# Four tokens per partition, input gate on GpSimd, scan input in fp32 PSUM: a gated linear recurrence on one core

## The chip, the cores and the metric

The kernel runs on one core of a Trainium2 chip. The metric is the device time of one execution in microseconds (us), the median of repeated runs. A profiled execution gives the views quoted here. Its span is some 2 us shorter than the time of the same run. The engines are PE (matmul), DVE (VectorE), ACT (ScalarE), POOL (GpSimd) and the 16 DMA engines; PEld is PE's weight load.

## The reference, cut to what matters

There are 4 sequences of 6336 tokens with 256 channels, in fp32.

```python
sig_r, sig_i = sigmoid(r_gate), sigmoid(i_gate)
a_t  = exp(8 * sig_r * log(a_base))                # decay per token and channel
xg   = sqrt(max(1 - a_t**2, 1e-6)) * sig_i * x
h    = a_t[:, t] * h + xg[:, t];  y[:, t] = h      # for every t
gate = sigmoid(causal_conv5(y))                    # 5 taps per channel
out  = (gate * (y @ w_val)) @ w_out
```

## The kernel before

The 25344 tokens are cut into 49 windows of 512 and one of 256. A window is loaded with tokens on partitions. PE transposes it so that channels lie on partitions and tokens along the row, and DVE then scans along the row. A static plan, made from a table of estimated durations (`COST`), fixes each engine's order. Rings of 11 windows lie between the front (load, tanh, exp, square) and the back (scan, convolution, output). The parts that matter here are:

```python
# load: token j*128 + p of the window goes to partition p: pieces of 1 KB
nc.sync.dma_start(dst, src[t0:t0 + nj * P, :].rearrange("(j p) d -> p j d", p=P))
...
# input gate, DVE: (tanh(i/2) + 1) * x, both operands in SBUF
nc.vector.scalar_tensor_tensor(out=uring[...], in0=tri[:, 1, ...], scalar=1.0, in1=xt[...], op0=ALU.add, op1=ALU.mult)
# square of the decay, GpSimd
nc.gpsimd.tensor_tensor(out=ering[...], in0=a, in1=a, op=ALU.mult)
# gating, DVE: transposed input (PSUM, bf16) times norm (SBUF, bf16) -> SBUF, bf16
nc.vector.tensor_tensor(out=xg[...], in0=uT[...], in1=nh[...], op=ALU.mult)
# scan, DVE, per half of the channels: decay (SBUF) and gated input (SBUF)
nc.vector.tensor_tensor_scan(out=yb[:, h, ...], data0=aring[...], data1=xg[:, h, c0:c1], initial=..., op0=ALU.mult, op1=ALU.add)
...
# final gate, DVE: (tanh + 1) * value, contiguous
nc.vector.scalar_tensor_tensor(out=gv[...], in0=tg[...], scalar=1.0, in1=val[...], op0=ALU.add, op1=ALU.mult)
# output product, PE: 128 tokens of gv are the weights
nc.tensor.matmul(out=ops[:, e, :], lhsT=gv[:, hk, p0:p0 + P], rhs=wo2[:, hk, :], ...)
```

## Time and profile before

| | before |
|---|---|
| time, median of the first 3 runs | 375.75 us (374.08 to 376.87) |
| span of the profiled run | 372.5 us |
| DVE, ACT, PE, POOL busy | 334.6, 312.4, 272.4, 138.3 us |
| DMA packets, share of 16 engines' span | 105160; main queue 85.7% |

The lines are shown in the prediction. In a group line the columns are the source line, engine, operation, output and input names with their shapes, and the count. After the first bar come the busy sum in us and the mean ns of one. After the second bar comes the engine's idle time just before these instructions, with what ended most of it. In the slice view each digit is the busy share of one fortieth of the span, in tenths.

### The profile page before, as it was taken

Reading aid. Unit: us, or ns where it says so; the run is one execution under the profiler, and the core shown is the slowest. Engines: PE = TensorE matmul, PEld = TensorE weight load, DVE = VectorE, ACT = ScalarE, POOL = GpSimd, SP = SyncE. Lnnn points to the kernel's source line nnn. Section 1 sums busy time; section 2 is a strip of 40 time slices with the busy share of each in tenths; the row PEclk is TensorE's granted clock in tenths of the full one; section 3 lists DMA queues with packets and bytes.
Section 4 is the critical chain, followed back from the end, with each engine's and each line's share of the span. In section 5 each row is a group of like instructions: output and inputs, shape, how many; then the busy total and the mean of one; then the engine's idle time right before and its main releaser. Section 6 shows DMA issues by size and latency. Waiting matters only on the chain.

```text
span 372.5 us, 5299 instructions
## 1 busy us (share of the span) xinstructions
PE 272.4 (73%) x1933; PEld 159.9 (43%) x1933; DVE 334.6 (90%) x326; ACT 312.4 (84%) x298; POOL 138.3 (37%) x111
## 2 busy tenths in 40 slices
PE   0362779877686969877677887696976696869994
PEld 0232445444445535434344454363543363435543
DVE  3363999999999979999999999999999999999982
ACT  4898899999998799998967989789997997873342
POOL 2234435634362726434425324451655056300000
PEclk9995699999899899999889989789999899999998
DMA  8999996999999989996889979979999895313333
GB/s 210 355 348 353 356 350 201 298 353 339 345 361 324 330 268 361 352 364 202 280 264 339 351 226 295 356 255 344 301 323 336 278 340 187 127 56 114 113 114 141
DMA packets 105160, 104.42 MB, mean 280 GB/s; under 512 B 3240, under 2 KB 105135, under 8 KB 105135
## 3 DMA queue, kind: packets, MB, share of 16 engines
q1 hardware_dynamic: 104590, 103.83, 85.7%
q0 software_dynamic: 544, 0.26, 0.5%
q8 instruction: 15, 0.25, 0.3%
q14 instruction: 11, 0.08, 0.1%
HBM read 78.39 MB, written 25.95 MB: 280 GB/s over the span
## 4 chain that ended last, share of the span: by engine, by line
DVE 34%; ACT 23%; issue 19%; PE 14%; DMA 5%; POOL 2%; DVEq 0%; ACTq 0%
DVE yring L306 13%; DVE uring L246 8%; DVE gv L344 7%; ACT tri L240 6%; ACT ering L277 5%; PE gp L321 5%; PE ops L356 4%; ACT aring L257 4%; DMA xt<-in_x_dram 3%; DVE xg L290 3%; PE val L338 3%; ACT tg L327 3%; DVE osb L367 2%; ACT L327 2%; ACT L277 2%
## 5 line engine op out<-in xcount | busy, mean ns | idle before, releaser
L262 POOL TENSOR_TENSOR ering<-aring 128x1024 f32<-128x1024 f32 (+1 forms) x50 | 105.7, 2121 | 140.9 <-ACT aring L257 121.8
L321 PE MATMUL gp<-yring,diag 128*128 128x512 bf16 (+4 forms) x530 | 124.5, 384 | 24.7 <-DVE yring L306 14.2
L306 DVE TENSOR_TENSOR_SCAN yring<-aring,yring,xg 128x512 bf16<-128x512 f32 (+4 forms) x98 | 139.5, 1464 | 0.7
L240 ACT ACTIVATE tri<-ri 128x2048 bf16<-128x2048 f32 (+1 forms) x50 | 94.4, 1907 | 0.0
L321 PEld LDWEIGHTS <-diag 128*128 128x128 bf16 x530 | 50.8, 102 | 83.5 <-issue 16.3
L356 PE MATMUL ops<-wo,gv 128*128 128x256 bf16 x396 | 61.8, 280 | 26.2 <-DVE gv L344 12.4
L257 ACT ACTIVATE aring<-srT,khf 128x512 f32<-128x512 bf16 (+1 forms) x100 | 71.8, 791 | 3.4 <-PE srT L228 2.2
L246 DVE SCALAR_TENSOR_TENSOR uring<-tri,xt 128x1024 bf16<-128x1024 bf16 (+1 forms) x50 | 67.4, 1356 | 7.0 <-ACT tri L240 6.9
L327 ACT ACTIVATE tg<-gp 128x1024 bf16<-128x1024 f32 (+1 forms) x50 | 51.1, 1023 | 25.7 <-PE gp L321 21.2
L344 DVE SCALAR_TENSOR_TENSOR gv<-tg,val 128x1024 bf16<-128x1024 bf16 (+1 forms) x50 | 59.7, 1194 | 2.5 <-PE val L338 1.7
L304 POOL COPY yring<-yring 128x8 bf16<-128x8 bf16 x49 | 31.6, 644 | 77.4 <-DVE yring L306 77.4
L356 PEld LDWEIGHTS <-gv 128*128 128x128 bf16 x396 | 36.7, 99 | 50.0 <-DVE gv L344 20.2
L338 PE MATMUL val<-yring,wv 128*128 128x512 bf16 (+4 forms) x212 | 52.1, 371 | 5.3 <-DVE gv L344 5.3
L228 PE MATMUL srT<-ident_b,tri 128*128 128x128 bf16 x396 | 33.4, 232 | 22.2 <-ACT tri L240 22.2
L277 ACT ACTIVATE ering<-ering,b 128x3072 bf16<-128x3072 f32 (+2 forms) x21 | 47.0, 2280 | 0.1
L369 ACT COPY osb<-ops 128x512 f32<-128x512 f32 x46 | 27.2, 592 | 22.2 <-PE ops L356 19.1
L367 DVE COPY osb<-ops 128x512 f32<-128x512 f32 x53 | 36.1, 682 | 9.2 <-PE ops L356 8.0
L228 PE MATMUL uT<-ident_b,uring 128*128 128x128 bf16 x396 | 33.3, 232 | 15.0 <-DVE xg L290 14.7
L228 PEld LDWEIGHTS <-tri 128*128 128x128 bf16 x396 | 27.0, 104 | 33.2 <-ACT tri L240 27.1
L290 DVE TENSOR_TENSOR xg<-uT,ering 128x1024 bf16<-128x1024 bf16 (+1 forms) x50 | 33.7, 675 | 6.2 <-ACT ering L277 6.2
L228 PEld LDWEIGHTS <-uring 128*128 128x128 bf16 x396 | 28.3, 104 | 20.0 <-issue 14.3
L338 PEld LDWEIGHTS <-wv 128*128 128x128 bf16 x212 | 19.9, 99 | 18.9 <-issue 6.6
(31 smaller groups left out, 53.3 us busy)
## 6 DMA issues: line engine op xcount, KB each, us to landing
ri<-in_r_gate_dram SPq DMA_DIRECT2D x49, 512.0 KB, 6.1
ri<-in_i_gate_dram SPq DMA_DIRECT2D x49, 512.0 KB, 7.4
xt<-in_x_dram SPq DMA_DIRECT2D x49, 512.0 KB, 7.3
out_dram<-osb SPq DMA_DIRECT2D x49, 512.0 KB, 4.6
ri<-in_r_gate_dram SPq DMA_DIRECT2D x1, 256.0 KB, 7.0
ri<-in_i_gate_dram SPq DMA_DIRECT2D x1, 256.0 KB, 7.2
xt<-in_x_dram SPq DMA_DIRECT2D x1, 256.0 KB, 6.6
out_dram<-osb SPq DMA_DIRECT2D x1, 256.0 KB
```

Of the source, the lines that this page charges most:

```text
L228: nc.tensor.transpose(out=dst[:, h, j * P:(j + 1) * P], in_=src[:, j, h * P:(h + 1) * P], identity=ident_b[:])
L240: nc.scalar.activation(out=tri[:, :, 0:nj, :], in_=ri[:, :, 0:nj, :], func=ACT.Tanh, scale=0.5)
L246: nc.vector.scalar_tensor_tensor(out=uring[:, g % NS, 0:nj, :], in0=tri[:, 1, 0:nj, :], scalar=1.0, in1=xt[:, 0:nj, :], op0=ALU.add, op1=A ...
L257: nc.scalar.activation(out=aring[:, g % NS, h, 0:ntok[g]], in_=srT[:, h, 0:ntok[g]], func=ACT.Exp, scale=khf[:, h:h + 1], bias=khf[:, h:h ...
L262: nc.gpsimd.tensor_tensor(out=ering[:, g % NS, :, 0:ntok[g]], in0=a, in1=a, op=ALU.mult)
L277: nc.scalar.activation(out=nring[:, sl:sl + k, 0:H * WIN], in_=ering[:, sl:sl + k].rearrange("p s h t -> p s (h t)"), func=ACT.Sqrt, scale ...
L306: nc.vector.tensor_tensor_scan(out=yb[:, h, o:o + c1 - c0], data0=aring[:, g % NS, h, c0:c1], data1=xg[:, h, c0:c1], initial=0.0 if fresh ...
L321: nc.tensor.matmul(out=gp[:, h, c0:c1], lhsT=diag[:, h, kk, :], rhs=yb[:, h, o:o + c1 - c0], start=(kk == 0), stop=(kk == CONV_K - 1))
L327: nc.scalar.activation(out=tg[:, :, 0:ntok[g]], in_=live.pop(("gp", g))[:, :, 0:ntok[g]], func=ACT.Tanh, scale=0.5)
L338: nc.tensor.matmul(out=val[:, m, c0:c1], lhsT=wv[:, hk, m * P:(m + 1) * P], rhs=yb[:, hk, o:o + c1 - c0], start=(hk == 0), stop=(hk == H - 1))
L344: nc.vector.scalar_tensor_tensor(out=gv[:, :, 0:ntok[g]], in0=live.pop(("tg", g))[:, :, 0:ntok[g]], scalar=1.0, in1=live.pop(("val", g))[: ...
L356: nc.tensor.matmul(out=ops[:, e, :], lhsT=gv[:, hk, p0:p0 + P], rhs=wo2[:, hk, :], start=(hk == 0), stop=(hk == H - 1))
```

## The change

The intent was to take the input gate off the fullest engine, to free the scan from its delays beside GpSimd (in the kernel before a pair of scans takes 4.04 us beside a square and 2.45 us with GpSimd idle), to load and store pieces of 4 KB, and to drop small copies at the ring's seams.

- Partition p now holds four successive tokens, so pieces are 4 KB. PE's transposes then deliver tokens permuted, and three later operations read or write with a step to put them in order and back.
- The input gate becomes two GpSimd instructions.
- The gating is split in halves and writes fp32 to PSUM, where the scan reads it.
- The y ring is contiguous, so the convolution reads over the seam and the four-column copies go.

```diff
-            nc.sync.dma_start(dst, src[...].rearrange("(j p) d -> p j d", p=P))
+            nc.sync.dma_start(dst, src[...].rearrange("(p j) d -> p j d", j=nj))
...
-            nc.vector.scalar_tensor_tensor(out=uring[...], in0=tri[:, 1, 0:nj, :], scalar=1.0,
-                                           in1=xt[:, 0:nj, :], op0=ALU.add, op1=ALU.mult)
+            t1 = work.tile([P, SUB, D], FP32, name="t1", tag="t1", bufs=1)
+            nc.gpsimd.tensor_scalar(out=t1[...], in0=tri[:, 1, 0:nj, :], scalar1=1.0, scalar2=None, op0=ALU.add)
+            nc.gpsimd.tensor_tensor(out=uring[...], in0=t1[...], in1=xt[...], op=ALU.mult)
...
-            srT = psum.tile([P, H, WIN], BF16, name="srT", tag="srT", bufs=2)
+            srT = psum.tile([P, H, WIN], BF16, name="srT", tag="srT", bufs=1)
...
+            for h in range(H):
+                xg = psum.tile([P, WIN], FP32, name="xg", tag="xg", bufs=1)
+                nc.vector.tensor_tensor(out=xg[...], in0=by_token(uT, h, g), in1=nring[...], op=ALU.mult)
...
-            gv = work.tile([P, H, WIN], BF16, name="gv", tag="gv", bufs=2)
-            nc.vector.scalar_tensor_tensor(out=gv[...], in0=tg[...], scalar=1.0, in1=val[...], ...)
+            gv = work.tile([P, SUB, H, P], BF16, name="gv", tag="gv", bufs=2)
+                nc.vector.scalar_tensor_tensor(
+                    out=gv[:, 0:nj, hs, :].rearrange("c j h p -> c (h p) j"),
+                    in0=tg[:, hs, ...].rearrange("c h (p j) -> c (h p) j", j=nj), scalar=1.0,
+                    in1=val[:, hs, ...].rearrange("c h (p j) -> c (h p) j", j=nj), op0=ALU.add, op1=ALU.mult)
```

Cut: the ring's index arithmetic, the split convolution at the seam, the load, store and exp patterns, and the new `COST` values.

More of the change, by code (lines that the diff above doesn't have):

```diff
@@ L19 @@
 MIN_UNIT = [1, 2, 3, 4]
-COST = dict(load=4.5, tanh=1.9, u2=1.3, srT=0.5, uT=0.5, exp=1.45, e=2.15, xg=0.66, scan=2.7, conv=2.4, tg=0.97,
-            val=0.95, gv=1.16, out=0.47, osbD=0.64, osbA=0.62, sq=0.88, sq0=0.2, table=1.3, store=1.5,
+COST = dict(load=3.9, tanh=1.9, u2=3.3, srT=0.5, uT=0.5, exp=1.45, e=2.15, scan=3.75, conv=2.45, tg=1.0,
+            val=0.95, gv=1.2, out=0.5, osbD=0.68, osbA=0.6, sq=0.88, sq0=0.2, table=1.3, store=1.3,
             sem=0.15, dma=2.2)
@@ L67, in make_plan @@
         per_window("tanh", "ACT", 3, [("load", 0), ("srT", -NTRI), ("u2", -NTRI)])
-        per_window("u2", "DVE", 0, [("tanh", 0), ("uT", -NS)])
-        per_window("srT", "PE", 0, [("tanh", 0), ("exp", -2)])
+        per_window("u2", "POOL", 1, [("tanh", 0), ("uT", -NS)])
+        per_window("srT", "PE", 0, [("tanh", 0), ("exp", -1)])
         per_window("exp", "ACT", 1, [("srT", 0), ("scan", -NS), ("e", -NS)])
-        per_window("e", "POOL", 0, [("exp", 0), ("xg", -NS)])
-        per_window("uT", "PE", 1, [("u2", 0), ("xg", -1)], nsq)
-        per_window("xg", "DVE", 3, [("uT", 0), ("sq", 0), ("scan", -1)], nsq)
-        per_window("scan", "DVE", 2, [("xg", 0), ("val", -NY)], nsq)
+        per_window("e", "POOL", 0, [("exp", 0), ("scan", -NS)])
+        per_window("uT", "PE", 1, [("u2", 0), ("scan", -1)], nsq)
+        per_window("scan", "DVE", 2, [("uT", 0), ("sq", 0), ("val", -NY), ("conv", 1 - NY)], nsq)
         per_window("conv", "PE", 3, [("scan", 0), ("tg", -1)])
@@ L97, in make_plan @@
                                               and at("exp") >= NS)
-            low = (nsq - at("scan")) * (COST["xg"] + COST["scan"]) <= 2 * COST["table"] + COST["sq"] * n
+            low = (nsq - at("scan")) * (COST["scan"]) <= 2 * COST["table"] + COST["sq"] * n
             enough = n >= min(MIN_UNIT[min(len(units), len(MIN_UNIT) - 1)], nw - nsq)
@@ L151 @@
         segs.append([(c0 - t0, c1 - t0, c0 % S == 0) for c0, c1 in zip(cuts[:-1], cuts[1:])])
-    YW = WIN + 4 * max(len(s) for s in segs)
     plan, qwin = make_plan([n / WIN for n in ntok])
@@ L165, in load @@
         for dst, src in ((ri[:, 0, 0:nj, :], rf), (ri[:, 1, 0:nj, :], if_), (xt[:, 0:nj, :], xf)):
-            nc.sync.dma_start(dst, src[t0:t0 + nj * P, :].rearrange("(j p) d -> p j d", p=P))
+            nc.sync.dma_start(dst, src[t0:t0 + nj * P, :].rearrange("(p j) d -> p j d", j=nj))
         live["ri", g], live["xt", g] = ri, xt
@@ L222 @@
         uring = rings.tile([P, NS, SUB, D], BF16, name="uring")
-        yring = rings.tile([P, NY, H, YW], BF16, name="yring")
+        yring = rings.tile([P, H, NY * WIN], BF16, name="yring")
         def transposes(dst, src, g):
@@ L245, in op_u2, with by_token @@
             xt, tri = live.pop(("xt", g)), live["tri", g]
-            nc.vector.scalar_tensor_tensor(out=uring[:, g % NS, 0:nj, :], in0=tri[:, 1, 0:nj, :], scalar=1.0,
-                                           in1=xt[:, 0:nj, :], op0=ALU.add, op1=ALU.mult)
+            t1 = work.tile([P, SUB, D], FP32, name="t1", tag="t1", bufs=1)
+            nc.gpsimd.tensor_scalar(out=t1[:, 0:nj, :], in0=tri[:, 1, 0:nj, :], scalar1=1.0, scalar2=None, op0=ALU.add)
+            nc.gpsimd.tensor_tensor(out=uring[:, g % NS, 0:nj, :], in0=t1[:, 0:nj, :], in1=xt[:, 0:nj, :],
+                                    op=ALU.mult)
         def op_srT(g, eng, n):
-            srT = psum.tile([P, H, WIN], BF16, name="srT", tag="srT", bufs=2)
+            srT = psum.tile([P, H, WIN], BF16, name="srT", tag="srT", bufs=1)
             transposes(srT, live["tri", g][:, 0], g)
             live["srT", g] = srT
+        def by_token(t, h, g):
+            return t[:, h, 0:ntok[g]].rearrange("c (j p) -> c p j", p=P)
         def op_exp(g, eng, n):
             srT = live.pop(("srT", g))
+            nj = ntok[g] // P
             for h in range(H):
-                nc.scalar.activation(out=aring[:, g % NS, h, 0:ntok[g]], in_=srT[:, h, 0:ntok[g]], func=ACT.Exp,
+                nc.scalar.activation(out=aring[:, g % NS, h, 0:ntok[g]].rearrange("c (p j) -> c p j", j=nj),
+                                     in_=by_token(srT, h, g), func=ACT.Exp,
                                      scale=khf[:, h:h + 1], bias=khf[:, h:h + 1])
@@ L285, in op_uT @@
             live["uT", g] = uT
-        def op_xg(g, eng, n):
-            xg = work.tile([P, H, WIN], BF16, name="xg", tag="xg", bufs=2)
-            nh = nring[:, g % NS, 0:H * WIN].rearrange("p (h t) -> p h t", h=H)
-            nc.vector.tensor_tensor(out=xg[:, :, 0:ntok[g]], in0=live.pop(("uT", g))[:, :, 0:ntok[g]],
-                                    in1=nh[:, :, 0:ntok[g]], op=ALU.mult)
-            live["xg", g] = xg
-        def op_scan(g, eng, n):
-            xg = live.pop(("xg", g))
-            yb = yring[:, g % NY]
-            py = yring[:, (g - 1) % NY]
-            pend = ntok[g - 1] + 4 * len(segs[g - 1]) if g else 0
-            for s, (c0, c1, fresh) in enumerate(segs[g]):
-                o = c0 + 4 + 4 * s
-                if fresh:
-                    nc.gpsimd.memset(yb[:, :, o - 4:o], 0.0)
-                else:
-                    nc.gpsimd.tensor_copy(out=yb[:, :, o - 4:o], in_=py[:, :, pend - 4:pend])
-                for h in range(H):
+        def op_scan(g, eng, n):
+            uT = live.pop(("uT", g))
+            nj = ntok[g] // P
+            y0 = g % NY * WIN
+            yp = (g - 1) % NY * WIN + (ntok[g - 1] if g else 0) - 1
+            for h in range(H):
+                xg = psum.tile([P, WIN], FP32, name="xg", tag="xg", bufs=1)
+                nc.vector.tensor_tensor(
+                    out=xg[:, 0:ntok[g]].rearrange("c (p j) -> c p j", j=nj), in0=by_token(uT, h, g),
+                    in1=nring[:, g % NS, h * WIN:h * WIN + ntok[g]].rearrange("c (p j) -> c p j", j=nj),
+                    op=ALU.mult)
+                for (c0, c1, fresh) in segs[g]:
                     nc.vector.tensor_tensor_scan(
-                        out=yb[:, h, o:o + c1 - c0],
+                        out=yring[:, h, y0 + c0:y0 + c1],
                         data0=aring[:, g % NS, h, c0:c1],
-                        data1=xg[:, h, c0:c1],
-                        initial=0.0 if fresh else py[:, h, pend - 1:pend],
+                        data1=xg[:, c0:c1],
+                        initial=0.0 if fresh else yring[:, h, yp:yp + 1],
                         op0=ALU.mult, op1=ALU.add,
@@ L314, in op_conv @@
         def op_conv(g, eng, n):
-            yb = yring[:, g % NY]
             gp = psum.tile([P, H, WIN], FP32, name="gp", tag="gp", bufs=1)
+            y0 = g % NY * WIN
+            yend = NY * WIN
             for h in range(H):
-                for s, (c0, c1, fresh) in enumerate(segs[g]):
-                    for kk in range(CONV_K):
-                        o = c0 + 4 * s + kk
-                        nc.tensor.matmul(out=gp[:, h, c0:c1], lhsT=diag[:, h, kk, :], rhs=yb[:, h, o:o + c1 - c0],
-                                         start=(kk == 0), stop=(kk == CONV_K - 1))
+                for kk in range(CONV_K - 1, -1, -1):
+                    sh = CONV_K - 1 - kk
+                    parts = []
+                    for (c0, c1, fresh) in segs[g]:
+                        if fresh:
+                            parts.append((c0 + sh, c1, y0 + c0))
+                        elif y0 + c0 >= sh:
+                            parts.append((c0, c1, y0 + c0 - sh))
+                        else:
+                            parts.append((0, sh, yend - sh))
+                            parts.append((sh, c1, y0))
+                    if sh == 0:
+                        parts = [(0, ntok[g], y0)]
+                    for k, (c0, c1, src) in enumerate(parts):
+                        nc.tensor.matmul(out=gp[:, h, c0:c1], lhsT=diag[:, h, kk, :],
+                                         rhs=yring[:, h, src:src + c1 - c0],
+                                         start=(sh == 0), stop=(kk == 0 and k == len(parts) - 1))
             live["gp", g] = gp
@@ L331, in op_val @@
         def op_val(g, eng, n):
-            yb = yring[:, g % NY]
+            y0 = g % NY * WIN
             val = psum.tile([P, H, WIN], FP32, name="val", tag="val", bufs=1)
             for m in range(H):
-                for s, (c0, c1, fresh) in enumerate(segs[g]):
-                    for hk in range(H):
-                        o = c0 + 4 * s + 4
-                        nc.tensor.matmul(out=val[:, m, c0:c1], lhsT=wv[:, hk, m * P:(m + 1) * P],
-                                         rhs=yb[:, hk, o:o + c1 - c0], start=(hk == 0), stop=(hk == H - 1))
+                for hk in range(H):
+                    nc.tensor.matmul(out=val[:, m, 0:ntok[g]], lhsT=wv[:, hk, m * P:(m + 1) * P],
+                                     rhs=yring[:, hk, y0:y0 + ntok[g]], start=(hk == 0), stop=(hk == H - 1))
             live["val", g] = val
         def op_gv(g, eng, n):
-            gv = work.tile([P, H, WIN], BF16, name="gv", tag="gv", bufs=2)
-            nc.vector.scalar_tensor_tensor(out=gv[:, :, 0:ntok[g]], in0=live.pop(("tg", g))[:, :, 0:ntok[g]],
-                                           scalar=1.0, in1=live.pop(("val", g))[:, :, 0:ntok[g]],
-                                           op0=ALU.add, op1=ALU.mult)
+            gv = work.tile([P, SUB, H, P], BF16, name="gv", tag="gv", bufs=2)
+            tg, val = live.pop(("tg", g)), live.pop(("val", g))
+            nj = ntok[g] // P
+            for hs in ([slice(0, H)] if nj == SUB else [slice(h, h + 1) for h in range(H)]):
+                nc.vector.scalar_tensor_tensor(
+                    out=gv[:, 0:nj, hs, :].rearrange("c j h p -> c (h p) j"),
+                    in0=tg[:, hs, 0:ntok[g]].rearrange("c h (p j) -> c (h p) j", j=nj), scalar=1.0,
+                    in1=val[:, hs, 0:ntok[g]].rearrange("c h (p j) -> c (h p) j", j=nj), op0=ALU.add, op1=ALU.mult)
             live["gv", g] = gv
@@ L353, in op_out @@
             for e in range(2):
-                p0 = (2 * i + e) * P
                 for hk in range(H):
-                    nc.tensor.matmul(out=ops[:, e, :], lhsT=gv[:, hk, p0:p0 + P], rhs=wo2[:, hk, :],
+                    nc.tensor.matmul(out=ops[:, e, :], lhsT=gv[:, 2 * i + e, hk, :], rhs=wo2[:, hk, :],
                                      start=(hk == 0), stop=(hk == H - 1))
@@ L372, in op_store @@
             nj = ntok[g] // P
-            nc.sync.dma_start(of[g * WIN:g * WIN + nj * P, :].rearrange("(j p) d -> p j d", p=P),
+            nc.sync.dma_start(of[g * WIN:g * WIN + nj * P, :].rearrange("(p j) d -> p j d", j=nj),
                               live.pop(("osb", g))[:, 0:nj, :])
         ops_by_name = dict(load=op_load, tanh=op_tanh, u2=op_u2, srT=op_srT, exp=op_exp, e=op_e, sq=op_sq,
-                           uT=op_uT, xg=op_xg, scan=op_scan, conv=op_conv, tg=op_tg, val=op_val, gv=op_gv,
+                           uT=op_uT, scan=op_scan, conv=op_conv, tg=op_tg, val=op_val, gv=op_gv,
                            out=op_out, osb=op_osb, store=op_store)
```

## The prediction

> **What bounds the kernel now.** I read the page's busy shares first, then the slices over time, then the groups by line, then the waits of the busiest engine, then its timeline. Busy shares:
>
> ```profile
> span 372.5 us, 5299 instructions
> PE 272.4 (73%) x1933; PEld 159.9 (43%) x1933; DVE 334.6 (90%) x326; ACT 312.4 (84%) x298; POOL 138.3 (37%) x111
> ...
> DVE  3363999999999979999999999999999999999982
> ACT  4898899999998799998967989789997997873342
> POOL 2234435634362726434425324451655056300000
> ...
> DMA  8999996999999989996889979979999895313333
> ```
>
> DVE is full from the fifth slice to the end. ACT and DMA are nearly full too, but only for the first 80%: the last 50 us are DVE working off a backlog (the ring lets the front run up to 11 windows ahead) while ACT is at 3 to 4 tenths and the loads are over. DVE's waits are small: the longest sums are 8.0 us (output copies, for PE), 6.9 us (input gate, for tanh) and 6.2 us (gating, for the square root). About 18 us of its 38 us idle is the head, before the first scan. So **DVE bounds it, with ACT 22 us of work behind**. The groups say what DVE does, and what the others would have to carry:
>
> ```profile
> L306 DVE TENSOR_TENSOR_SCAN yring<-aring,yring,xg 128x512 bf16<-128x512 f32 (+4 forms) x98 | 139.5, 1464 | 0.7
> ...
> L246 DVE SCALAR_TENSOR_TENSOR uring<-tri,xt 128x1024 bf16<-128x1024 bf16 (+1 forms) x50 | 67.4, 1356 | 7.0 <-ACT tri L240 6.9
> ...
> L344 DVE SCALAR_TENSOR_TENSOR gv<-tg,val 128x1024 bf16<-128x1024 bf16 (+1 forms) x50 | 59.7, 1194 | 2.5 <-PE val L338 1.7
> ...
> L367 DVE COPY osb<-ops 128x512 f32<-128x512 f32 x53 | 36.1, 682 | 9.2 <-PE ops L356 8.0
> ...
> L290 DVE TENSOR_TENSOR xg<-uT,ering 128x1024 bf16<-128x1024 bf16 (+1 forms) x50 | 33.7, 675 | 6.2 <-ACT ering L277 6.2
> ```
>
> These five sum to 336.4 us. The timeline of two stretches shows why the scan's mean is not its own time (columns: start, duration, what):
>
> ```profile
> 92.52 4.04 DVE L306 TENSOR_TENSOR_SCAN yring<-aring,yring,xg 128x512 bf16<-128x512 f32 x2
> ...
> 92.87 2.61 POOL L262 TENSOR_TENSOR ering<-aring 128x1024 f32<-128x1024 f32 x1 [2.33 <-ACT aring L257]
> ...
> 349.72 2.45 DVE L306 TENSOR_TENSOR_SCAN yring<-aring,yring,xg 128x512 bf16<-128x512 f32 x2
> ...
> 121.08 4.72 POOL L262 TENSOR_TENSOR ering<-aring 128x1024 f32<-128x1024 f32 x2 [3.95 <-ACT aring L257]
> 122.12 0.68 DVE L367 COPY osb<-ops 128x512 f32<-128x512 f32 x1
> 123.65 1.22 DVE L344 SCALAR_TENSOR_TENSOR gv<-tg,val 128x1024 bf16<-128x1024 bf16 x1 [0.86 <-PE val L338]
> 124.79 0.69 DVE L290 TENSOR_TENSOR xg<-uT,ering 128x1024 bf16<-128x1024 bf16 x1
> ```
>
> A pair of scans takes 2.45 us when GpSimd is idle and 4.04 us beside one GpSimd square; the square takes 2.61 us instead of its median 1.89. Another pair, beside two squares, took 5.75 us. The DVE operations with a PSUM operand (output copy 0.68, final gate 1.22, gating 0.69) keep their idle-GpSimd times beside a square.
>
> [...] The gating now, all bf16, takes 0.675 us for 1024 elements, which is a doubled rate; the final gate with an fp32 PSUM operand takes 1.19, single rate. [...] Nothing in the kernel before hops, [...] the change does hop, on the PSUM reads of exp and gating and on the SBUF write of the final gate. This is my main doubt.
>
> **The change, part by part.**
>
> *DVE.* The input gate goes: minus 67.4 us. The gating becomes two instructions of 512 elements with fp32 output, single rate. The final gate's two sizes (1204 ns at 1024, 677 ns at 512) give 1.03 ns per element and 0.15 us fixed, so 0.68 us each; 99 of them are 67 us against 33.7: plus 34. The scan has one SBUF and one PSUM operand, so it should take 1.22 us whatever GpSimd does: 49.5 windows x 2.43 = 120 against 139.5: minus 19. Final gate and copies stay at first. Sum: 336 - 67 + 34 - 19 = **284 us**. The scan now follows directly on the gating it reads; in the timeline that step is 0.70 us from start to start where 0.60 is normal, so 2 x 0.1 x 49.5 adds 10 us of small gaps: 294 us occupied.
>
> *ACT.* Nothing added or removed: **312 us**, if strided PSUM reads are free for exp. It is thus the fuller one. But the plan hands output copies to whichever engine is free first; ACT has 46 of them at 0.59 us (27 us), each costing 0.68 on DVE. Moving some 20 gives ACT 300 and DVE 308 occupied. Both near 300 is the best split, which I take.
>
> *GpSimd.* It keeps the squares and loses 49 four-column copies (31.6 us, mostly contention by their 0.19 to 1.2 us). It gains a one-input pass [...] and a two-input pass of the square's size (1.9 us). [...]
>
> *PE.* Same columns, plus small wrap pieces once in seven windows: 272 us busy. Its wait for the four-column copies goes. But the transpose buffer of the recurrence gate drops to one, so it must be emptied by exp before the next is filled.
>
> *DMA.* Today a packet of about 1 KB takes 0.857 x 372.5 x 16 / 104590 = 48.8 ns, so at the best slices' 355 GB/s the 104.4 MB need 294 us. That would be a second wall at exactly the new length. [...] The pieces protect the gain more than they make one.
>
> *Sum.* ACT's first work is at 7.6 us and window 0 needs until about 18 us for its first scan; that head stays. At the end, the backlog tail (ACT at a third for 50 us) should shrink to the chain of the last windows, estimate 12 us at light load. In between ACT and DVE have 300 us each. In the stretch from 40 to 320 us DVE alone is the wall now and is 97% busy, while ACT idles 9%. With two engines equally loaded, static order and single PSUM buffers, neither hides the other's waits: I take 7%, 22 us. 7.6 + 300 + 12 + 22 = 342 us span. The timed median lies 3 us over the profiled span now, so **344 us**, 8% less.
>
> **The rivals.**
> *A: hopping costs.* [...] DVE then occupies 330 to 360 us, and the time is 360 to 385: nearly nothing won, or a small loss. Against it: [...] the plan's own constants in the change keep final gate at 1.2 and exp at 1.45, which are the durations of the trace before; an author who retuned them after a run would have seen such a cost. I give it one in five.
> *B: a new wait takes the place of the removed work.* The input gate is now a GpSimd pair queued with squares, it holds the x buffer longer, and loads come later; or the single transpose buffers tie PE, ACT and DVE in step. For it: four engines between 240 and 305 us and in-order queues. Against it: an 11-window ring still decouples front and back, and GpSimd has a fifth of its time free. It would make 350 to 362.
> *C: DMA stays the wall.* If 4 KB pieces were no faster, 294 us plus head and tail is some 320, still below 344; it would only bite jointly with B, for 350.
> *D: better than thought.* If the waits stay at DVE's 3% of today, 325 to 332.
>
> **Range and chances.** The centre is 344; D sets the low end at 328, B and the mild half of A the high end at 366. Faster by over 2% means below 368: 0.84. Within 2% needs most of A: 0.10. Slower than 383 needs A in full, or A with B: 0.06.
>
> **What would show it.** Right: scan mean near 1.22 us with GpSimd over 65% busy; gating 0.68 us x99; no input gate on DVE; final gate still 1.2, exp pair unchanged; DVE and ACT each 290 to 310 us busy, with more copies on DVE than 53; ACT busy nearly to the end; packets near 26,000 with a DMA share below 80%. Wrong: gating above 0.85 or final gate above 1.5 us (A); scans still above 1.4 us (contention not gone); ACT waits for transposes or loads, or DVE waits for the transposed input, summing to over 40 us (B); GpSimd passes of more than 5.5 us per window, making it the bound.

GpSimd's work came to 238 us, for a square, a one-input pass and a two-input pass in each window; what the text says of GpSimd's load rests on that sum. Rival A's outcome is left (330 to 360 us of DVE, a time of 360 to 385), but what it put on the hopping write and reads is cut; to hop is to step away at every element. The single rate for fp32 output was the estimate from the final gate's 1.19 us with an fp32 PSUM operand; a later run shows it (gating 0.69 us for 512 elements in gvread, against 0.68 for 1024 before).

## More of the kernel before

All timed runs that are compared are in the fast state; one slow run of the kernel before (379.58 us) is left out of the ratios of its round. The kernels ran in four rounds, in which the median of the kernel before lay between 374.91 and 377.12 us, so a difference of times taken across rounds is good to some 2 us.

## The result, and the profile after

The changed kernel takes **519.64 us** (518.84 to 520.4, 4 runs). The kernel before takes 374.91 us in the same rounds. The ratio is 1.385 (95% interval 1.378 to 1.392): **38% slower**. Here and below a ratio is the mean time of one kernel's fast runs over that of the other's of the same rounds, so it is not quite the ratio of the quoted medians.

The page of the changed kernel, busy shares and slices:

```profile
span 517.1 us, 5526 instructions
PE 322.3 (62%) x1971; PEld 181.2 (35%) x1971; DVE 451.9 (87%) x320; ACT 325.3 (63%) x312; POOL 347.8 (67%) x158
...
DVE  3243999978999979999989999999999979999993
ACT  6969667498665774847575685597476594365221
POOL 4999969969965965948773986957948859400000
...
DMA  8975754869845467457755774575845651201112
```

DVE still bounds the kernel, with 117 us more work instead of 50 us less. ACT is only two thirds busy and DMA is light. POOL carries 348 us where 238 had been expected. The groups of lines, answering those shown of before:

```profile
L356 DVE SCALAR_TENSOR_TENSOR gv<-tg,val 128x1024 bf16<-128x1024 bf16 (+1 forms) x51 | 232.9, 4574 | 10.7 <-ACT tg L338 5.1
L267 POOL TENSOR_TENSOR ering<-aring 128x1024 f32<-128x1024 f32 (+1 forms) x50 | 93.8, 1878 | 94.3 <-ACT aring L261 90.0
L245 POOL TENSOR_SCALAR t<-tri 128x1024 f32<-128x1024 bf16 (+1 forms) x50 | 137.2, 2745 | 20.8 <-ACT tri L238 16.2
...
L304 DVE TENSOR_TENSOR_SCAN yring<-aring,yring,xg 128x512 bf16<-128x512 f32 (+4 forms) x98 | 120.6, 1231 | 3.5
...
L246 POOL TENSOR_TENSOR uring<-t,xt 128x1024 bf16<-128x1024 f32 (+1 forms) x50 | 116.7, 2334 | 4.2
...
L299 DVE TENSOR_TENSOR xg<-uT,ering 128x512 f32<-128x512 bf16 (+1 forms) x100 | 76.0, 760 | 20.1 <-ACT ering L282 15.0
```

One line holds most of it: the final gate takes 4.57 us on average where it took 1.19, and 232.9 us in all where it took 59.7. That is 173 us of DVE work of which the prediction's sum had nothing and its rival A too little (330 to 360 us of DVE in all). (The record of an instruction behind the gate starts some 0.4 us before the gate's ends, so records overlap, and the groups add up to more than the 451.9 us in which DVE is busy.) The scan is where the prediction had it, at 1.23 us. The GpSimd pass that adds one takes 2.75 us, and its multiply 2.33 us. The timeline of DVE shows that the gate's length is steady and needs no neighbour to explain it (columns: start, duration, what):

```profile
205.79 1.28 DVE L304 TENSOR_TENSOR_SCAN yring<-aring,yring,xg 128x512 bf16<-128x512 f32 x1
206.98 4.70 DVE L356 SCALAR_TENSOR_TENSOR gv<-tg,val 128x1024 bf16<-128x1024 bf16 x1
211.30 0.90 DVE L379 COPY osb<-ops 128x512 f32<-128x512 f32 x1
...
484.98 4.68 DVE L356 SCALAR_TENSOR_TENSOR gv<-tg,val 128x1024 bf16<-128x1024 bf16 x1
```

The gate at 206.98 runs beside GpSimd work. The one at 484.98 runs when GpSimd has had its last instruction 17 us before, at 466.76 to 467.80. Both take 4.7 us.

### The profile page after: what moved, and what is told of

The parts are those of the page before. It is cut to its first block, busy times and chain, and to the rows that moved or that the text cites. A ratio compares the mean times of both kernels' runs of the same rounds, so it can differ in the third digit from the quotient of the medians.

```text
span 517.1 us, 5526 instructions
## 1 busy us (share of the span) xinstructions
PE 322.3 (62%) x1971; PEld 181.2 (35%) x1971; DVE 451.9 (87%) x320; ACT 325.3 (63%) x312; POOL 347.8 (67%) x158
## 2 busy tenths in 40 slices
DMA packets 29386, 104.44 MB, mean 202 GB/s; under 512 B 3239, under 2 KB 3758, under 8 KB 29358
## 3 DMA queue, kind: packets, MB, share of 16 engines
q1 hardware_dynamic: 28814, 103.83, 55.9%
## 4 chain that ended last, share of the span: by engine, by line
DVE 45%; issue 31%; PE 12%; ACT 4%; DMA 4%; SPq 0%; DVEq 0%; ACTq 0%
DVE gv L356 19%; DVE yring L304 11%; DVE xg L299 10%; DVE osb L379 4%; PE ops L368 4%; DMA out_dram<-osb 3%; PE gp L331 3%; PE val L347 3%; ACT tri L238 2%; PE uT L226 1%; DMA ri<-in_i_gate_dram 1%; PE srT L226 1%; ACT aring L261 1%; ACT osb L381 0%; ACT ering L282 0%
## 5 line engine op out<-in xcount | busy, mean ns | idle before, releaser
L356 DVE SCALAR_TENSOR_TENSOR gv<-tg,val 128x1024 bf16<-128x1024 bf16 (+1 forms) x51 | 232.9, 4574 | 10.7 <-ACT tg L338 5.1
L267 POOL TENSOR_TENSOR ering<-aring 128x1024 f32<-128x1024 f32 (+1 forms) x50 | 93.8, 1878 | 94.3 <-ACT aring L261 90.0
L245 POOL TENSOR_SCALAR t<-tri 128x1024 f32<-128x1024 bf16 (+1 forms) x50 | 137.2, 2745 | 20.8 <-ACT tri L238 16.2
L331 PE MATMUL gp<-yring,diag 128*128 128x512 bf16 (+13 forms) x580 | 143.8, 402 | 4.3 <-DVE yring L304 4.2
L304 DVE TENSOR_TENSOR_SCAN yring<-aring,yring,xg 128x512 bf16<-128x512 f32 (+4 forms) x98 | 120.6, 1231 | 3.5
L368 PE MATMUL ops<-wo,gv 128*128 128x256 bf16 x396 | 76.1, 327 | 72.3 <-DVE gv L356 37.9
L246 POOL TENSOR_TENSOR uring<-t,xt 128x1024 bf16<-128x1024 f32 (+1 forms) x50 | 116.7, 2334 | 4.2
L347 PE MATMUL val<-yring,wv 128*128 128x512 bf16 (+1 forms) x200 | 65.1, 459 | 61.4 <-DVE gv L356 61.4
L299 DVE TENSOR_TENSOR xg<-uT,ering 128x512 f32<-128x512 bf16 (+1 forms) x100 | 76.0, 760 | 20.1 <-ACT ering L282 15.0
L331 PEld LDWEIGHTS <-diag 128*128 128x128 bf16 x580 | 59.2, 112 | 74.4 <-issue 36.3
```

The costliest lines, as they stand in the source:

```text
L245: nc.gpsimd.tensor_scalar(out=t1[:, 0:nj, :], in0=tri[:, 1, 0:nj, :], scalar1=1.0, scalar2=None, op0=ALU.add)
L246: nc.gpsimd.tensor_tensor(out=uring[:, g % NS, 0:nj, :], in0=t1[:, 0:nj, :], in1=xt[:, 0:nj, :], op=ALU.mult)
L267: nc.gpsimd.tensor_tensor(out=ering[:, g % NS, :, 0:ntok[g]], in0=a, in1=a, op=ALU.mult)
L299: nc.vector.tensor_tensor(out=xg[:, 0:ntok[g]].rearrange("c (p j) -> c p j", j=nj), in0=by_token(uT, h, g), in1=nring[:, g % NS, h * WIN:h ...
L304: nc.vector.tensor_tensor_scan(out=yring[:, h, y0 + c0:y0 + c1], data0=aring[:, g % NS, h, c0:c1], data1=xg[:, c0:c1], initial=0.0 if fres ...
L331: nc.tensor.matmul(out=gp[:, h, c0:c1], lhsT=diag[:, h, kk, :], rhs=yring[:, h, src:src + c1 - c0], start=(sh == 0), stop=(kk == 0 and k = ...
```

## The experiments

Twelve kernels ran. The theory after the result: two terms of the sum had been mis-sized, the hopping bf16 write of the final gate and the GpSimd pass that adds one, and the second was hidden behind the first. The rivals: the write as the whole loss; the reads with a step; a new wait from the single transpose buffer or the GpSimd queue; DMA.

### Single operations at the end of the kernel before (mb)

After the last store, three of each form were appended, each on a line of its own. `ms` is bf16 in SBUF, `mps` fp32 in PSUM, and the outputs lie in rings no longer in use.

```diff
+        for _ in range(REPS):   # L406: contiguous
+            nc.vector.scalar_tensor_tensor(**stt(oflat[:, 0:1024], *src))
+        for _ in range(REPS):   # L408: the changed kernel's write, step 512 bytes
+            nc.vector.scalar_tensor_tensor(**stt(oflat[:, 0:1024].rearrange("c (j p) -> c p j", j=4), *sj))
+        for _ in range(REPS):   # L412: contiguous write, reads with a step of four elements
+            nc.vector.scalar_tensor_tensor(**stt(oflat[:, 0:1024].rearrange("c (j p) -> c j p", j=4), *jo))
...                              # L410 step 576 bytes, L416 fp32 step 1024, L418 bf16 step 8, L430 bf16 step 32, L433 runs of 4 bytes
```

> The kernel before with a tail of single operations appended, three of each, to time forms by themselves (the result stays right; the total is a little longer and does not matter). Final-gate form, 1024 elements: contiguous write 1.2 us. Theory W (it is the hopping bf16 write): the write with a 512-byte step 4.7 us, the same write at a 528-byte step much less if it is a bank conflict and the same 4.7 if any hop does it; hopping reads with a contiguous write under 1.6 us. Theory R (it is the whole four-way permutation, reads included): contiguous write with hopping reads also above 3 us. fp32 write with a 1024-byte step: below 2.5 us if the cost belongs to 2-byte writes, 4.7 if to the hop. Runs of 4 and 8 bytes should fall towards 1.2 us. GpSimd: bf16 to fp32 add of a constant 2.77 us as in the changed kernel; fp32 to fp32 [...] 2.7 us if tensor-scalar is slow as such; bf16-output multiply 2.35 us against 1.9 us with fp32 output.

One correction to that text: the rows of the second form turned out 576 bytes apart, not 528. The groups of the appended lines (this answer keeps different shapes apart):

```profile
L408 DVE SCALAR_TENSOR_TENSOR ering<-aring,gp 128x1024 bf16<-128x1024 bf16 x3 | 14.1, 4702 | 0.1
L410 DVE SCALAR_TENSOR_TENSOR ering<-aring,gp 128x1024 bf16<-128x1024 bf16 x3 | 13.8, 4593 | 0.1
...
L430 DVE SCALAR_TENSOR_TENSOR aring<-aring,gp 128x1024 bf16<-128x1024 bf16 x3 | 13.3, 4430 | 0.1
L449 POOL TENSOR_SCALAR ering<-aring 128x1024 f32<-128x1024 f32 x3 | 8.3, 2771 | 0.2
L445 POOL TENSOR_SCALAR ering<-aring 128x1024 f32<-128x1024 bf16 x3 | 8.3, 2771 | 116.2 <-DVE aring L441 116.0
...
L418 DVE SCALAR_TENSOR_TENSOR ering<-aring,gp 128x1024 bf16<-128x1024 bf16 x3 | 7.2, 2416 | 0.1
...
L416 DVE SCALAR_TENSOR_TENSOR ering<-aring,gp 128x1024 f32<-128x1024 bf16 x3 | 5.7, 1892 | 0.1
...
L433 DVE SCALAR_TENSOR_TENSOR aring<-aring,gp 128x1024 bf16<-128x1024 bf16 x3 | 3.7, 1221 | 0.1
...
L412 DVE SCALAR_TENSOR_TENSOR ering<-aring,gp 128x1024 bf16<-128x1024 bf16 x3 | 3.7, 1220 | 0.1
...
L406 DVE SCALAR_TENSOR_TENSOR ering<-aring,gp 128x1024 bf16<-128x1024 bf16 x3 | 3.6, 1201 | 0.1
...
L459 POOL CAST ering<-aring 128x1024 f32<-128x1024 bf16 x3 | 3.1, 1040 | 0.2
```

The write by itself costs 4.70 us against 1.20. Another row pitch hardly changes it (4.59), and a step of 32 bytes takes 4.43, so a conflict peculiar to 512 bytes is out. Single 2-byte elements far apart are the worst: with a step of 8 bytes they take 2.42, and fp32 elements with a step of 1024 bytes take 1.89 (1.22 contiguous). Bf16 elements written two at a time, in runs of 4 bytes 64 bytes apart, take 1.22, as if contiguous, and so do runs of 8 bytes. An fp32 write with a step of 1024 bytes that goes to PSUM takes 1.23. Reads with a step of four elements are free (1.22 against 1.20). So theory W holds and theory R falls. Why a lone 2-byte write costs that much is not shown.

In the same run GpSimd's tensor-scalar takes 2.77 us in all three pairs of types tried (bf16 to fp32, bf16 to bf16, fp32 to fp32), while its plain cast from bf16 to fp32 takes 1.04. So the bf16 input is not what costs, and the case that stands in the expectation holds: the tensor-scalar form is slow as such. The last forecast missed: the multiply of one tensor with itself takes 1.89 us with bf16 output too, not 2.35, so the type of the output does not explain the changed kernel's 2.33 (mb3 below does).

### The final gate with its loops turned (gvread)

```diff
-                    out=gv[:, 0:nj, hs, :].rearrange("c j h p -> c (h p) j"),
-                    in0=tg[...].rearrange("c h (p j) -> c (h p) j", j=nj), scalar=1.0,
-                    in1=val[...].rearrange("c h (p j) -> c (h p) j", j=nj), ...)
+                    out=gv[:, 0:nj, hs, :].rearrange("c j h p -> c j (h p)"),
+                    in0=tg[...].rearrange("c h (p j) -> c j (h p)", j=nj), scalar=1.0,
+                    in1=val[...].rearrange("c h (p j) -> c j (h p)", j=nj), ...)
```

> The change with only the loop order of the final gate turned: it writes contiguously and reads its two inputs with a step of four elements. Theory 1 (the hopping write was the whole loss): gate 1.2 to 1.6 us, DVE about 285 us busy, time about 345. Theory 2 (mine: two terms failed; GpSimd at 1.9 + 2.77 + 2.35 = 7.0 us a window is the next wall): time 375 to 395, GpSimd above 85% busy, DVE about 75%. Theory 3 (hopping reads cost as much): gate above 3 us, time above 450.

It takes 396.35 us; the ratio to the kernel before is 1.050 (1.044 to 1.056). The page of this kernel, busy shares and slices:

```profile
PE 275.4 (70%) x1971; PEld 165.7 (42%) x1971; DVE 283.5 (72%) x320; ACT 322.1 (82%) x312; POOL 346.8 (88%) x158
...
POOL 2999999999999999999999999999999999994000
```

DVE has 283.5 us of work: the prediction's sum was 284. The final gate is at 1.18 us. Three swapped index letters take away 123 us, but the kernel is still slower than the one before, and the slices show why: GpSimd is full from the second slice to the thirty-sixth. The time lies 1.35 us above the range of theory 2; theories 1 and 3 are far off. The plan here still takes the input gate for 3.3 us on GpSimd, where it takes 5.1; a version planned with the right figure was not run.

### The un-permuting left to the weight loads (gvpe), and no layout change at all (nolayout)

```diff
# gvpe: gate in token order as in the kernel before, and in the output product
-                    nc.tensor.matmul(out=ops[:, e, :], lhsT=gv[:, 2 * i + e, hk, :], ...)
+                    nc.tensor.matmul(out=ops[:, e, :], lhsT=gv[:, hk, 0:ntok[g]].rearrange("c (p j) -> c p j", p=P)[:, :, 2 * i + e], ...)
# nolayout: besides the gate in token order, loads and stores as before, patterns of exp and gating contiguous
-            nc.sync.dma_start(dst, src[...].rearrange("(p j) d -> p j d", j=nj))
+            nc.sync.dma_start(dst, src[...].rearrange("(j p) d -> p j d", p=P))
```

> The change with the final gate in token order, all contiguous, and the un-permuting read left to the weight loads of the output product (step of four elements). Gate 1.2 us as in the kernel before. If weight loads hop freely, the same 375 to 395 us as the version with hopping reads (GpSimd wall); if they do not, weight loads above 0.2 us each and PE busy by more than 40 us longer. Theory 1 says 345.

> The change without its layout part: 1 KB pieces as before and no un-permuting anywhere; GpSimd gating, fp32 PSUM scan input and the contiguous ring stay. Scan 1.22, gating 0.68, gate 1.2 us. GpSimd wall: 375 to 395, equal within 2% to the two versions with 4 KB pieces, so that the pieces would be worth nothing here. DMA as a second wall: over 2% slower than they are, with a DMA share above 85%. Theory 1: 345.

They take 396.74 us (ratio 1.051) and 398.01 us (ratio 1.055). With a step of four elements a weight load of the output product takes 114 ns against 98 in gvread, which costs no time here. Without any layout change the kernel is 0.4% slower than with it, with a DMA share of 79.9% against 73.4%. So the other stepped accesses cost nothing either: the gating takes 0.691 us with its stepped PSUM read (gvread) and 0.692 without, exp 0.788 and 0.784. Both times are again a little above their range, and all three versions meet the same wall.

### The add of one taken off GpSimd, with both layouts (v2_4k, v2_1k)

Both have the contiguous gate write. DVE adds the one in place in bf16, and GpSimd only multiplies. v2_1k is the same upon nolayout. `COST` has the new entries.

```diff
+            nc.vector.tensor_scalar(out=t, in0=t, scalar1=1.0, scalar2=None, op0=ALU.add)      # t = tri[:, 1, 0:nj, :]
-            nc.gpsimd.tensor_scalar(out=t1[...], in0=tri[:, 1, 0:nj, :], scalar1=1.0, scalar2=None, op0=ALU.add)
-            nc.gpsimd.tensor_tensor(out=uring[...], in0=t1[...], in1=xt[...], op=ALU.mult)
+            nc.gpsimd.tensor_tensor(out=uring[...], in0=tri[:, 1, 0:nj, :], in1=xt[...], op=ALU.mult)
```

> The change with the contiguous final-gate write, and the add of one (GpSimd tensor-scalar, 2.77 us) moved to DVE as an in-place bf16 tensor-scalar (0.43 us by the copy of that form timed alone); GpSimd keeps the square and one multiply, near 1.9 + 2.2 = 4.1 us a window, 205 us. DVE 283 + 21 = 305 us, ACT 322. If the oversized GpSimd pass was the only second failure, the balanced picture of the prediction returns: 340 to 358 us, 5 to 10% below the kernel before. If a new wait (single transpose buffers, GpSimd queue) holds it, 360 to 385.

> The same with 1 KB pieces and no un-permuting anywhere. With 104 MB moved in some 350 us and 49 ns a packet, the DMA share would be near 90%. If the pieces matter once the engines no longer bind: 2% or more slower than the 4 KB version. If not: within 1%.

They take 370.07 us (ratio 0.984, interval 0.976 to 0.991) and 371.80 us (ratio 0.987, interval 0.981 to 0.993). These are the only correct versions whose median is more than 1% below the kernel before. The page of v2_4k:

```profile
PE 273.5 (74%) x1939; PEld 164.4 (45%) x1971; DVE 312.0 (85%) x370; ACT 320.9 (87%) x312; POOL 202.1 (55%) x108
```

GpSimd is out of the way, at the 205 us expected. But the time fell into the second range, not the 340 to 358 hoped for. DVE got the one-adding as 32.3 us instead of 21: it took 0.66 us on average where it takes 0.41 alone (below). The trace shows contention with GpSimd:

```profile
23.15 0.40 DVE L245 TENSOR_SCALAR tri<-tri 128x1024 bf16<-128x1024 bf16 x1
24.31 1.74 DVE L245 TENSOR_SCALAR tri<-tri 128x1024 bf16<-128x1024 bf16 x1 [0.76 <-ACT tri L239]
...
23.63 2.13 POOL L250 TENSOR_TENSOR uring<-tri,xt 128x1024 bf16<-128x1024 bf16 x1 [3.26 <-DVE tri L245]
```

All 15 of these that the timeline lists singly and with no GpSimd instruction beside them (overlapping in time) take 0.40 to 0.42 us; those beside one take 0.43 to 2.00. Together DVE and ACT have 633 us of work, which is 633 / 2 = 316 each, and each idles some 50 us of the 368. No single wait carries that; the largest of ACT is 24 us for PE's convolution. The two layouts differ by less than their intervals, although the DMA share is 85.6% with 1 KB pieces and 76.0% with 4 KB. The layout part, with the gate's write mended, is thus worth about half a per cent here, at the edge of the noise.

### The input gate back on DVE (gatedve)

```diff
-            nc.gpsimd.tensor_scalar(out=t1[...], ...)
-            nc.gpsimd.tensor_tensor(out=uring[...], in0=t1[...], in1=xt[...], op=ALU.mult)
+            nc.vector.scalar_tensor_tensor(out=uring[...], in0=tri[:, 1, 0:nj, :], scalar=1.0, in1=xt[...], op0=ALU.add, op1=ALU.mult)
```

> The change with the contiguous final-gate write and the whole input gate back on DVE as one instruction of 1.2 to 1.4 us; GpSimd keeps only the square, 94 us. DVE 283 + 65 = 348 us. Theory of work sums: DVE bound, 372 to 390 us, within 2% or a little above the kernel before, so that moving the gate was worth having only with a cheaper form. If it is below 365, the GpSimd gate was a mistake altogether.

It takes 389.25 us (ratio 1.033, interval 1.027 to 1.039) with 340.4 us of DVE work at 88%: DVE bound, at the top of the range. Taken with v2_4k, splitting the gate is worth 19 us against leaving it whole on DVE. Put whole on GpSimd (gvread), it loses 7 us. The run also shows the rest of the change, its write mended, with the input gate where it was: it is 3% slower than the kernel before. On DVE the gating with fp32 output takes 69.1 us where it took 33.7, and the scan gives back only 18.9 of that (120.6 against 139.5).

### GpSimd and DVE forms alone, continued (mb3)

```diff
+            nc.gpsimd.tensor_tensor(out=mh, in0=mf[:], in1=mf[:], op=ALU.mult)     # L416, one tensor twice
+            nc.gpsimd.tensor_tensor(out=mh, in0=mf[:], in1=mk, op=ALU.mult)        # L418, two fp32 tensors
+            nc.vector.tensor_scalar(out=ms[:], in0=ms[:], scalar1=1.0, scalar2=None, op0=ALU.add)   # L410
```

> The kernel before with a tail of single operations: GpSimd multiply of one tensor with itself 1.89 us, of two different fp32 tensors 2.35 us if the second stream costs by itself (the 2.35 of the changed kernel is then its own time), 1.9 if that was contention; bf16 times fp32 2.13; bf16 plus bf16 2.1 to 2.4; tensor-scalar with multiply 2.77 as with add; with 512 elements 1.4 to 1.5. DVE bf16 add of a constant 0.43 us, in place and out of place.

The groups of three of the appended lines:

```profile
L418 POOL TENSOR_TENSOR ering<-aring 128x1024 bf16<-128x1024 f32 x3 | 7.0, 2338 | 0.2
...
L416 POOL TENSOR_TENSOR ering<-aring 128x1024 bf16<-128x1024 f32 x3 | 5.7, 1892 | 35.9 <-DVE aring L414 35.8
...
L410 DVE TENSOR_SCALAR aring<-aring 128x1024 bf16<-128x1024 bf16 x3 | 1.2, 406 | 0.1
```

A GpSimd multiply of two different fp32 tensors takes 2.34 us by itself. The 1.89 us of the square, which reads one tensor twice, was the wrong row to size it by. Bf16 times fp32 takes 2.13. Tensor-scalar with a multiply takes 2.78 and with 512 elements 1.49, all as expected. DVE's add of one takes 0.41 us in place.

### The kernel that the prediction had summed (ideal)

The add of one is left out, so the result is wrong, but the two mis-sized terms are gone and nothing is added elsewhere. The plan's cost for the gate is set to 2.2. The prediction's sum had an add of one on GpSimd too, so this GpSimd (199.5 us) is lighter than the 238 predicted.

```diff
-            nc.gpsimd.tensor_scalar(out=t1[...], in0=tri[:, 1, 0:nj, :], scalar1=1.0, scalar2=None, op0=ALU.add)
-            nc.gpsimd.tensor_tensor(out=uring[...], in0=t1[...], in1=xt[...], op=ALU.mult)
+            nc.gpsimd.tensor_tensor(out=uring[...], in0=tri[:, 1, 0:nj, :], in1=xt[...], op=ALU.mult)
```

> Wrong result on purpose: the change with the contiguous final-gate write and the add of one left out altogether (GpSimd only multiplies). Both mis-sized terms are then gone and nothing is added elsewhere: DVE 283, ACT 322, GpSimd near 205 us. It is the kernel that the prediction summed. If its handling of waits was sound: 335 to 352 us. If the balanced engines lose more to each other than the 7% taken, or the split of the output copies does not shift: 353 to 368, and a third step failed.

It takes 350.86 us (ratio 0.935, interval 0.932 to 0.939).

```profile
span 348.6 us, 5462 instructions
PE 265.9 (76%) x1971; PEld 161.9 (46%) x1971; DVE 287.4 (82%) x329; ACT 315.6 (91%) x303; POOL 199.5 (57%) x108
```

This is within the prediction's range and 7 us above its centre. So its total for the head, the tail and the waits was about right, in part by luck (see below). Against v2_4k only DVE's add of one is gone, so that pass, with the wait that it puts before GpSimd's multiply, costs v2_4k 19 us.

### The hopping write in the good version (hop), larger square-root groups (units)

hop is v2_4k with the changed kernel's gate write; units is v2_4k with `MIN_UNIT = [1, 3, 5]` in place of `[1, 2, 3, 4]`.

> The version that beat the kernel before (370 us), with the hopping final-gate write of the change put back and GpSimd light. DVE 312 + 173 = 485 us. If the write alone makes the loss: 530 to 555 us, more than the change itself since DVE also adds the one. If part of the loss of the change came from the heavy GpSimd: below 520.

> The version with 370 us, with larger groups of square roots (1, 3, 5 in place of 1, 2, 3, 4): three fewer switches of the ACT table pair, 3 x 2.6 = 8 us less on ACT, which is the fuller engine (321 us). If ACT's sum sets the time: 358 to 366. If DVE starves at the start or between groups: 370 or more.

hop takes 539.02 us (ratio 1.435), with DVE at 474.4 us: with a light GpSimd the write alone makes the whole loss. units takes 373.98 us (ratio 0.996, interval 0.992 to 0.999): the second case of its expectation, 370 or more, and not 358 to 366. ACT's work fell by 6.5 us to 314.4, as intended, but the time did not follow: its ratio to the kernel before is worse than v2_4k's. In the traces ACT's waits for PE took the place: for the convolution 26.9 us (v2_4k 23.8), for the output product 13.3 (5.2), for the transposes 5.1 (1.5). Why PE delivers later was not settled.

### The scan's input in SBUF again (scansb)

```diff
-                xg = psum.tile([P, WIN], FP32, name="xg", tag="xg", bufs=1)
+                xg = work.tile([P, WIN], FP32, name="xg", tag="xg", bufs=1)
```

> The version with 370 us, with the gated input of the scan as fp32 in SBUF in place of PSUM; all else the same. Contention theory: scans that overlap GpSimd are held up; GpSimd is busy 55% of the time, so the mean scan rises from 1.23 to 1.5 us or more, GpSimd's operations also lengthen, and DVE-bound time rises by 25 us or more, to 390 to 420. Without contention: scans 1.23, time within 1% of 370.

It takes 416.67 us (ratio 1.110). The groups of this kernel:

```profile
L308 DVE TENSOR_TENSOR_SCAN yring<-aring,yring,xg 128x512 bf16<-128x512 f32 (+4 forms) x98 | 161.4, 1647 | 3.5
...
L271 POOL TENSOR_TENSOR ering<-aring 128x1024 f32<-128x1024 f32 (+1 forms) x50 | 113.3, 2266 | 59.5 <-ACT aring L265 41.5
```

Scans lengthen from 1.23 to 1.65 us and squares from 1.89 to 2.27. The lengthening is contention, and not the fp32 input in SBUF as such: of the 92 scans of 512 columns in this trace, the 34 with no GpSimd instruction beside them take 1.22 to 1.29 us, the 58 beside one up to 3.16, 1.93 on average. In v2_4k the 56 beside one take 1.22 to 1.28. So, with GpSimd carrying the multiply, PSUM is worth 47 us (416.67 less 370.07) against fp32 in SBUF. The kernel before had bf16 in SBUF, whose gating took 33.7 us in place of the 68.2 here; against that the gain would be smaller, and it was not run.

## Why the prediction was wrong, point by point

Two of the signs of being wrong that it named came true: a final gate above 1.5 us (4.57), and GpSimd passes above 5.5 us a window (347.8 / 49.5 = 7.0).

- **Scan, 1.22 us whatever GpSimd does: right.** It is 1.231 us (120.6 us in all), and scansb shows the contention that it escapes.
- **DVE's sum of 284 us: wrong by one term.** With the gate's write contiguous the profile has 283.5 (some 5 us of it by luck, since DVE did 46 copies and not 53). The step that failed is "Final gate and copies stay at first". The final gate measured 232.9 us instead of 59.7. Rival A named the hopping write, at one chance in five, and was also mis-sized: it came to 330 to 360 us of DVE, and the write alone added 173. Its terms rested on no trace. What mb shows is that the element's type matters: with a step of 1024 bytes an fp32 write takes 1.89 us, with 512 bytes a bf16 write 4.70. Its "against", that the plan's constants keep the gate at 1.2, was no evidence: the run contradicts the constant for this write.
- **Hopping reads: the doubt was needless.** Exp (0.788 with and 0.784 without a step) and gating (0.691 and 0.692) pay nothing.
- **ACT, "nothing added or removed", 312 us: 10 too few.** It is 322.1 in gvread: the new plan gave ACT 53 output copies instead of 46 (4.1 us more) and 31 loads of its function tables instead of 27 (1.28 us each).
- **GpSimd, 238 us: wrong.** Both added terms were too small. The multiply, put at 1.9 us, measured 2.33, which is (2.33 - 1.9) x 50 = 22 us of the 110 between 238 and the profile's 347.8. The other 88 are the one-input pass, which measured 2.75 and whose size in the sum rested on no trace. The multiply was sized by the square, which reads one tensor and takes 1.89 us, 1.6 times the 1.20 us of DVE's final gate; the multiply of two fp32 tensors takes 2.34, about twice. In the changed kernel all this was hidden behind DVE. It came up as the wall at 396 us once the write was mended.
- **DMA: direction right, weight small.** There are 29386 packets, and the share fell to 55.9% over a longer span. In gvread the packets take 290 us (0.734 x 395.0), in the kernel before 319. At 370 us 1 KB and 4 KB versions lie within half a per cent of each other. The second wall at 294 us was not tested: no 1 KB version ran near it.
- **PE, 272 us busy: right without the hop.** It is 275.4 in gvread. The 322.3 of the changed kernel came with a granted clock of 0.826 where the kernel before had 0.942.
- **Waits and split: the total nearly right, in part by luck.** The ideal kernel ran in 350.86 us against 344. The copies went 55 to DVE and 44 to ACT there (before: 53 and 46; in the changed kernel 46 and 53, the opposite of what was assumed), so ACT was not relieved; it kept 316 us instead of 300. It idled 33 us of the 348.6, where the prediction left 42 of 342. The two errors cancel but for 7 us.
- **Rival B, a new wait:** the single transpose buffers were no wall. In the ideal kernel ACT waits 0.3 us in all for the recurrence gate's transposes and DVE 1.6 us for the input's. Whether the GpSimd queue adds waits of its own, besides its work, is not separated.
- **DVE's idle head:** of the first 18 us DVE is busy for 6, so 12 and not 18 of its 38 idle us lie there. Nothing rests on it.

The account of the 176 us between 344 and 519.64, in the order of mending: the hopping write 123 (519.64 to 396.35), the whole GpSimd add of one 45 (396.35 to 350.86, with the plan's cost set anew), and 7 left over. The parts overlap: with the GpSimd wall gone the same write costs 169 us (hop 539.02 less v2_4k 370.07).

## What to carry to other kernels

When a change permutes data, put the step on a read (free for the bf16 and PSUM reads tried here: 1.22 us against 1.20 in mb) or keep at least two adjacent bf16 elements in each written run (1.22 us, where single ones took 2.42 to 4.70); here the order of three loop indices was worth 123 us. Size a moved operation by a row with the same form on the same engine, or time it alone before relying on it: a one-input pass on another engine is not a cheap one by default (the add of one took 2.77 us on GpSimd and 0.41 on DVE). After the first culprit is mended, look for the next full engine before calling the loss explained.
